# Whole-row runs for the weight loads of a decode block: wq, w_mod, w1 and w2 as consecutive rows per partition, activations transposed with a matching step

## Chip, cores, metric

One core of one Trainium2 chip. The metric is device microseconds of one execution. Of the 29 executions of the kernel before that are on record, 28 lie within 0.3% (703.12 to 704.98 us; the other took 706.48); a verdict of "faster" or "slower" needs 2%. A ratio below is the mean time of one kernel's fast runs over that of the other kernel's fast runs of the same rounds, so it is not quite the ratio of the medians that stand beside it.

In this document, MB are 10^6 bytes and KB 1024 bytes. Shares of a microsecond are read from single traces unless medians are named; traces of kernels with the same beginning agree there within about 0.3 us (w_mod's product starts at 21.27 to 21.59 us in five traces).

## The reference, cut to what matters

A transformer block in decode: 8 sequences, one new token each, D = 512, 32 query heads on 8 key/value heads, 8192 cached keys of 128 numbers, an MLP of 1792 hidden units with squared ReLU, all bf16.

```python
mod = silu(c) @ w_mod                      # [8,512] @ [512,3072] -> sa, ca, ga, sb, cb, gb
h = layernorm(x) * (1 + ca) + sa
q = h @ wq                                 # [8,512] @ [512,4096]
p = softmax(q . k_cache * Dh**-0.5)        # k_cache, v_cache: [8, 8, 8192, 128] each, 134 MB each
x = x + ga * ((p . v_cache) @ wo)          # wo: [4096,512]
h = layernorm(x) * (1 + cb) + sb
x = x + gb * (relu(h @ w1 + b1)**2 @ w2 + b2)   # w1: [512,1792], w2: [1792,512]
```

The caches are 268 MB of the 284 MB read. The four weights of the change are 11 MB.

## The kernel before

K and V come in 128 loads of 2 MB through a ring of eight slots, each partition getting one run of 16 KB. wq and w_mod borrow ring slots 6, 7 and 4, 5 at the start; w1 and w2 are the last two loads. PE (TensorE, the matrix engine; PEld is its loading of weights) transposes K, multiplies it with the queries, transposes the softmaxed scores P and multiplies them with V; VectorE and ScalarE (DVE and ACT in the profile) copy PE's results out.

The parts that the change touches:

```python
RING = [E0(nc.sbuf_tensor(f"ring{i}", [128, NT, DH], BF16)) for i in range(NSLOT)]
# ...
wq_r = A_wq.rearrange("(kt p) n -> p kt n", p=128)         # row kt*128+p on partition p
s_wq.inc(sp.dma_start(RINGF[6]..., wq_r[:, 0:2, :]), 16)    # 2 runs of 8 KB per partition
s_xc.inc(sp.dma_start(x_sb[:], A_x...), 16)
s_xc.inc(sp.dma_start(c_sb[:], c), 16)
s_wq.inc(sp.dma_start(RINGF[7]..., wq_r[:, 2:4, :]), 16)
wmod_r = w_mod.rearrange("(kt p) n -> p kt n", p=128)      # runs of 6 KB, two DMAs
# ...
for kt in range(KT_D):      # transposes of silu(c); the same for the two normalized rows, ha and hb
    ins = pe.matmul(csT_tp[:, kt, :], cs[:, kt * 128:(kt + 1) * 128], IDENT[0:B, 0:B], is_transpose=True)
# ...
for m in range(NLOADS):     # the load queue: wait for the slot, then issue
    # ... K, V: "(p t) d -> p t d", one run of 16 KB per partition
    # m == 4 also issues wo: A_wo.rearrange("(h dh) n -> dh h n"), 32 runs of 1 KB per partition
    # m == 128: B_w1.rearrange("(kt p) f -> p kt f", p=128)     4 runs of 3.5 KB
    # m == 129: B_w2.rearrange("(kt p) n -> p kt n", p=128)    14 runs of 1 KB
# ...
for hh, (f0, fl) in enumerate(FH):          # the hidden row, in two halves of 896
    s_dve.wait(pe, M_HSQH[hh])
    for kt in range(f0 // 128, (f0 + fl) // 128):
        ins = pe.matmul(hidT_tp[:, kt, :], hsq[:, kt * 128:(kt + 1) * 128], IDENT[0:B, 0:B], is_transpose=True)
    if hh == 0:
        pe_fill(pe, 10)                     # "fillers": matmuls whose result nobody reads
```

Of the kernel before, what the change touches and what calls it, by code (L numbers as in the profile page):

```python
# [9 lines left out]
BF16 = mybir.dt.bfloat16  # L10
# [17 lines left out]
def bass_adaLN_cond__gqa_block_cached__dense_activation_squared_relu__decode_kernel(  # L28
    nc, A_x, A_k_cache, A_v_cache, A_wq, A_wo, B_x, B_w1, B_b1, B_w2, B_b2, c, w_mod, out):
    B, _, D = A_x.shape  # L30
    _, HKV, SK, DH = A_k_cache.shape
    HQ = A_wq.shape[1] // DH
    REP = HQ // HKV
    F = B_w1.shape[1]
    NMOD = w_mod.shape[1]
    KT_D = D // 128
    KT_F = F // 128
    NCH = SK // 512
    NT = SK // 128
    NSLOT = 8  # L40
# [5 lines left out]
    with ExitStack() as es0:  # L46
        E0 = es0.enter_context
# [6 lines left out]
        IDENT = E0(nc.sbuf_tensor("IDENT", [128, 128], BF16))  # L54
# [21 lines left out]
        mv = E0(nc.sbuf_tensor("mv", [B, 2], FP32))  # L76
        std_ = E0(nc.sbuf_tensor("std_", [B, 1], FP32))
        rstd = E0(nc.sbuf_tensor("rstd", [B, 1], FP32))
        RING = [E0(nc.sbuf_tensor(f"ring{i}", [128, NT, DH], BF16)) for i in range(NSLOT)]
        RINGF = [r[:, :, :].rearrange("p t d -> p (t d)") for r in RING]  # L80

        WQ_SLOTS = (6, 7)
        WMOD_SLOTS = (4, 5)

        def wq_view(kt, h):
            r = RINGF[WQ_SLOTS[kt // 2]]
            base = (kt % 2) * (HQ * DH) + h * DH
            return r[:, base:base + DH]

        def wmod_view(kt, j):  # L90
            r = RINGF[WMOD_SLOTS[kt // 2]]
            base = (kt % 2) * NMOD + j * 512
            return r[:, base:base + 512]

        PS = E0(nc.psum_tensor("PS", [128, 8, 512], FP32))
        mod_ps = PS[0:B, 0:6, :]
# [1 line left out]
        csT_tp = tpro[:, 0:KT_D * B].rearrange("p (k b) -> p k b", k=KT_D)  # L98
        haT_tp = tpro[:, 32:32 + KT_D * B].rearrange("p (k b) -> p k b", k=KT_D)
# [12 lines left out]
        hbT_tp = PS[:, 7, :].bitcast(BF16)[:, 128:128 + KT_D * B].rearrange("p (k b) -> p k b", k=KT_D)  # L112
        hid_ps = PS[0:B, 0:4, :]
        hid_flat = hid_ps.rearrange("b k n -> b (k n)")
        hidT_tp = PS[:, 7, :].bitcast(BF16)[:, 0:KT_F * B].rearrange("p (k b) -> p k b", k=KT_F)
# [4 lines left out]
        s_wmod = S_("s_wmod")  # L120
        s_wq = S_("s_wq")
# [26 lines left out]
        def slot_of(m):  # L148
            return m % NSLOT, m // NSLOT

        def load_kind(m):
            if m >= 128:
                return ("w", m, 0)
            b, r = divmod(m, 16)
            return ("k", b, r) if r < 8 else ("v", b, r - 8)
        def v_uses_before(m):
            s = m % NSLOT
            return sum(1 for mm in range(s, m, NSLOT) if load_kind(mm)[0] == "v")

        def stg_k(b, g, j):  # L160
            return 72 * b + 8 * g + j
# [15 lines left out]
        def wait_evac(eng, seq):  # L177
            e, v = evac_ms[seq]
            (s_edve if e == "dve" else s_eact).wait(eng, v)
# [14 lines left out]
        cs = E1(nc.sbuf_tensor("cs", [B, D], BF16))  # L194
# [3 lines left out]
        ha = E1(nc.sbuf_tensor("ha", [B, D], BF16))  # L198
        haT = E1(nc.sbuf_tensor("haT", [128, KT_D, B], BF16))

        @block.sync
        def _(sp):
            wq_r = A_wq.rearrange("(kt p) n -> p kt n", p=128)
            s_wq.inc(sp.dma_start(RINGF[WQ_SLOTS[0]].rearrange("p (k n) -> p k n", k=2), wq_r[:, 0:2, :]), 16)
            s_xc.inc(sp.dma_start(x_sb[:], A_x.rearrange("b s d -> (b s) d")), 16)
            s_xc.inc(sp.dma_start(c_sb[:], c), 16)
            s_wq.inc(sp.dma_start(RINGF[WQ_SLOTS[1]].rearrange("p (k n) -> p k n", k=2), wq_r[:, 2:4, :]), 16)
            wmod_r = w_mod.rearrange("(kt p) n -> p kt n", p=128)
            s_wmod.inc(sp.dma_start(RINGF[WMOD_SLOTS[0]][:, 0:2 * NMOD].rearrange("p (k n) -> p k n", k=2), wmod_r[:, 0:2, :]), 16)
            s_wmod.inc(sp.dma_start(RINGF[WMOD_SLOTS[1]][:, 0:2 * NMOD].rearrange("p (k n) -> p k n", k=2), wmod_r[:, 2:4, :]), 16)  # L210
        V_XC = s_xc.n

        @block.gpsimd
# [57 lines left out]
        @block.tensor  # L271
        def _(pe):
            s_dve.wait(pe, M_CS)
            s_pool.wait(pe, M_CONSTS)
            for kt in range(KT_D):
                ins = pe.matmul(csT_tp[:, kt, :], cs[:, kt * 128:(kt + 1) * 128], IDENT[0:B, 0:B], is_transpose=True)  # L276
            s_pe.inc(ins)
        M_TPC = s_pe.n

# [33 lines left out]
        @block.tensor  # L313
        def _(pe):
            s_dve.wait(pe, M_HA)
            for kt in range(KT_D):
                ins = pe.matmul(haT_tp[:, kt, :], ha[:, kt * 128:(kt + 1) * 128], IDENT[0:B, 0:B], is_transpose=True)
            s_pe.inc(ins)
        M_TPH = s_pe.n

# [43 lines left out]
        @block.sync  # L364
        def _(sp):
            for m in range(NLOADS):
                s, u = slot_of(m)
                kind = load_kind(m)
                if u == 0:
                    if s in WQ_SLOTS:  # L370
                        s_pe.wait(sp, M_QT)
                    elif s in WMOD_SLOTS:
                        s_pe.wait(sp, M_MODMM)
                    if m == 4:
                        s_wo.inc(sp.dma_start(wo_sb[:], A_wo.rearrange("(h dh) n -> dh h n", dh=DH)), 16)
                        s_bb.inc(sp.dma_start(b1_row[:], B_b1.rearrange("(o f) -> o f", o=1)), 16)
                        s_bb.inc(sp.dma_start(b2_row[:], B_b2.rearrange("(o f) -> o f", o=1)), 16)
                else:
                    pk = load_kind(m - NSLOT)
                    if pk[0] == "k":  # L380
                        wait_evac(sp, stg_k(pk[1], pk[2], 7))
                    else:
                        assert pk[0] == "v"
                        s_free[s].wait(sp, v_uses_before(m))
                if kind[0] == "k":
                    src_ap = A_k_cache[kind[1], kind[2]].rearrange("(p t) d -> p t d", p=128)
                    dst_ap = RING[s][:, :, :]
                elif kind[0] == "v":
                    src_ap = A_v_cache[kind[1], kind[2]].rearrange("(p t) d -> p t d", p=128)
                    dst_ap = RING[s][:, :, :]  # L390
                elif m == LD_W1:
                    src_ap = B_w1.rearrange("(kt p) f -> p kt f", p=128)
                    dst_ap = W1v
                else:
                    src_ap = B_w2.rearrange("(kt p) n -> p kt n", p=128)
                    dst_ap = W2v
                ins = sp.dma_start(dst_ap, src_ap)
                if kind[0] in ("k", "v"):
                    s_ld[s].inc(ins, 16)
                elif m == LD_W1:  # L400
                    s_w1.inc(ins, 16)
                else:
                    s_w2.inc(ins, 16)
# [23 lines left out]
        for b in range(B):  # L427
            def T_tile(pe, b_, g_, j0=0, j1=8):
# [4 lines left out]
                for j in range(j0, j1):  # L433
# [3 lines left out]
                    for i in range(8):  # L437
                        t = 8 * j + i
                        ins = pe.matmul(STG[seq % NSTG][:, i, :], RING[s][:, t, :], IDENT[:, :], is_transpose=True)  # L439
                    v = s_stgw.inc(ins)  # L440
# [127 lines left out]
            def PV_group(pe, g):  # L568
# [6 lines left out]
                for t in range(NT):  # L575
                    if g == 0 and t % 8 == 0:
# [3 lines left out]
                                    Pm[:, t, 32 * qt + REP * g:32 * qt + REP * (g + 1)],  # L580
                                    RING[s][:, t, :], start=(t == 0), stop=(t == NT - 1),
                                    tile_position=(0, 32 * gq))
# [101 lines left out]
        hb = E3(nc.sbuf_tensor("hb", [B, D], BF16))  # L684
        hbT = E3(nc.sbuf_tensor("hbT", [128, KT_D, B], BF16))
        h1 = E3(nc.sbuf_tensor("h1", [B, F], BF16))
        hsq = E3(nc.sbuf_tensor("hsq", [B, F], BF16))
# [6 lines left out]
        def pe_fill(pe, n):  # L694
            for _ in range(n):
                pe.matmul(EFILL_ps, IDENT[:, :], IDENT[:, :])
# [33 lines left out]
        @block.tensor  # L730
        def _(pe):
            pe_fill(pe, 48)
            s_dve.wait(pe, M_HB)
            for kt in range(KT_D):
                ins = pe.matmul(hbT_tp[:, kt, :], hb[:, kt * 128:(kt + 1) * 128], IDENT[0:B, 0:B], is_transpose=True)
            s_pe.inc(ins)
            pe_fill(pe, 6)
        M_HBT = s_pe.n
# [34 lines left out]
        @block.tensor  # L773
        def _(pe):
            for hh, (f0, fl) in enumerate(FH):
                s_dve.wait(pe, M_HSQH[hh])
                for kt in range(f0 // 128, (f0 + fl) // 128):
                    ins = pe.matmul(hidT_tp[:, kt, :], hsq[:, kt * 128:(kt + 1) * 128], IDENT[0:B, 0:B], is_transpose=True)
                if hh == 0:
                    pe_fill(pe, 10)  # L780
            s_pe.inc(ins)
            pe_fill(pe, 6)
        M_HIDT = s_pe.n
# [59 lines left out]
```

## Time and profile before

| | before |
|---|---|
| time, median of 4 runs | 703.39 us (703.12 to 704.98) |
| bytes moved, packets | 285 MB, 26,109 |
| PE busy | 88% |
| last K load lands | 635.4 us |
| from there to the end | 66.3 us |

From the page of the kernel before: the span, PE's busy time, then two rows of 40 equal slices (busy share of the DMA engines in tenths, and GB/s), the packets by size, and the queue that fetches instructions.

```profile
span 701.7 us, 21480 instructions
PE 617.2 (88%) x10113; PEld 528.0 (75%) x10113; DVE 324.6 (46%) x594; ACT 177.7 (25%) x217; POOL 6.2 (1%) x25
...
DMA  9999999999999999999999999999999999999950
GB/s 354 430 372 429 423 427 425 424 425 428 428 423 425 427 427 424 427 425 426 425 425 426 425 427 423 428 427 424 427 425 425 423 430 424 426 426 427 412 208 1
DMA packets 26109, 285.05 MB, mean 406 GB/s; under 512 B 2187, under 2 KB 8100, under 8 KB 9125
...
q8 instruction: 80, 1.31, 0.8%
```

The DMA engines have no dry slice from the first to the last two. Note slice 2 (372 GB/s): that is where wo's 1 KB runs go through.

The view by stretches of the kernel before, stretches in us. The last two columns are the share of the DMA engines' time that was busy (over 1 where the times of packets overlap) and GB/s.

```profile
core 0: us, PE busy (x) PEld busy (x) DVE busy (x) ACT busy (x) POOL busy (x), PEclk, DMA share, GB/s
4.00:21.00 17.00, 0.26 (x4) 0.18 (x4) 2.09 (x6) 2.11 (x3) 3.13 (x13) 1.00 1.02 425
41.00:51.00 10.00, 10.00 (x147) 8.46 (x145) 7.57 (x12) 3.46 (x4) 0.00 (x0) 0.86 1.09 346
52.00:652.00 600.00, 546.85 (x9106) 473.57 (x9104) 298.03 (x530) 167.67 (x206) 0.00 (x0) 0.97 1.01 425
668.00:683.00 15.00, 15.00 (x257) 13.65 (x254) 1.85 (x9) 0.00 (x0) 0.00 (x0) 1.00 0.54 205
```

In the last row, w1 and w2 go through while only half of the DMA engines' time is used.

The chain of waits of the kernel before, in order of time (start, duration, what). These are two of its pieces: the wait for the last K load, and PE's first work on it.

```profile
598.51 36.87 DMA ring<-in_A_k_cache_dram
635.43 1.96 PE PS L439 x32
```

A piece of DMA in the chain runs from issue to landing, so it contains the time that the load stood in the queue. It ends at 598.51 + 36.87 = 635.38 us. Here the queue is never empty (no dry slice above), so the issue time does not matter (in experiment 7 PE starts on K 1.7 us later, and the last K lands at 634.75 us instead of 634.72); what matters is how much has to go through before.

The beginning, in the timeline of the kernel before (start, duration, engine, line, operation; in brackets the idle time before and what ended it):

```profile
9.02 0.63 ACT L244 ACTIVATE sig<-c_sb 8x512 f32<-8x512 bf16 x1 [6.93 <-DMA c_sb<-in_c_dram]
10.42 0.26 PE L276 MATMUL PS<-IDENT,cs 8*128 8x8 bf16 x4 [10.42 <-DVE cs L250]
21.33 8.02 PE L292 MATMUL PS<-ring,csT 128*8 128x512 bf16 x24 [10.65 <-DMA ring<-in_w_mod_dram]
```

PE waits for w_mod until 21.3 us; the activations were ready by 12.

The end, in the timeline of the kernel before: the second half of the squared hidden row, PE's transposes of the hidden row with ten fillers between, and VectorE's copy of the result.

```profile
693.55 0.61 DVE L771 TENSOR_TENSOR hsq<-h 8x896 bf16<-8x896 bf16 x1 [0.69 <-ACT h L766]
...
693.95 0.33 PE L778 MATMUL PS<-IDENT,hsq 8*128 8x8 bf16 x7
...
694.21 0.73 PE L696 MATMUL PS<-IDENT 128*128 128x128 bf16 x10
...
694.87 0.33 PE L778 MATMUL PS<-IDENT,hsq 8*128 8x8 bf16 x7
...
695.23 0.22 DVE L788 COPY hidT<-PS 128x112 bf16<-128x112 bf16 x1 [1.07 <-PE PS L778]
```

### The profile page before, as it was taken

The numbers are of one execution on the slowest core, as the hardware profiler recorded it, in microseconds if no ns is written. First come the engines' busy times: TensorE is split into PE (matmuls) and PEld (weight loads), VectorE is DVE, ScalarE is ACT, GpSimd is POOL, SyncE is SP. The second block draws the span as 40 slices with busy tenths as digits, with TensorE's granted clock in tenths as the row PEclk, the third lists the DMA queues.
The fourth block names the chain that finished last, engine by engine and source line by source line (L and its number), as shares of the span: only waits on it lengthen the run. The fifth ranks groups of instructions, "written<-read, shape, count | busy, mean of one in ns | idle before, by whom it ended". The sixth has DMA issues, their size and how long they took to land.

```text
span 701.7 us, 21480 instructions
## 1 busy us (share of the span) xinstructions
PE 617.2 (88%) x10113; PEld 528.0 (75%) x10113; DVE 324.6 (46%) x594; ACT 177.7 (25%) x217; POOL 6.2 (1%) x25
## 2 busy tenths in 40 slices
PE   0499799997989799997999899897989989997998
PEld 0187699776977699776987699776977689775984
DVE  1357612774057621766046720676027820676213
ACT  1024510443024410433013320344014420244101
POOL 3000000000000000000000000000000000000000
PEclk9979999999999899999999989999999999999999
DMA  9999999999999999999999999999999999999950
GB/s 354 430 372 429 423 427 425 424 425 428 428 423 425 427 427 424 427 425 426 425 425 426 425 427 423 428 427 424 427 425 425 423 430 424 426 426 427 412 208 1
DMA packets 26109, 285.05 MB, mean 406 GB/s; under 512 B 2187, under 2 KB 8100, under 8 KB 9125
## 3 DMA queue, kind: packets, MB, share of 16 engines
q1 hardware_dynamic: 26020, 283.68, 96.2%
q8 instruction: 80, 1.31, 0.8%
q14 instruction: 9, 0.07, 0.0%
HBM read 283.66 MB, written 0.01 MB: 404 GB/s over the span
## 4 chain that ended last, share of the span: by engine, by line
PE 49%; DMA 38%; DVE 10%; ACT 2%; issue 1%; SPq 0%
DMA ring<-in_A_k_cache_dram 30%; PE PS L439 23%; PE PS L579 14%; PE PS L477 6%; DMA ring<-in_A_v_cache_dram 5%; DVE KTb L413 5%; DMA ring<-in_w_mod_dram 3%; DVE m L501 2%; ACT P_sb L528 2%; PE PS L551 2%; PE PS L292 1%; PE PS L634 1%; PE PS L333 1%; DVE mod_sb L300 0%; PE PS L796 0%
## 5 line engine op out<-in xcount | busy, mean ns | idle before, releaser
L413 DVE COPY KTb<-PS 128x1024 bf16<-128x1024 bf16 x432 | 270.9, 684 | 80.7 <-PE PS L439 79.8
L439 PEld LDWEIGHTS PS<-IDENT,ring 128*128 128x128 bf16 x4096 | 230.7, 98 | 63.1 <-DMA ring<-in_A_k_cache_dram 35.3
L439 PE MATMUL PS<-IDENT,ring 128*128 128x128 bf16 x4096 | 251.2, 220 | 12.9 <-DMA ring<-in_A_k_cache_dram 11.8
L420 ACT ACTIVATE KTb<-PS 128x1024 bf16<-128x1024 bf16 x144 | 147.5, 1024 | 445.2 <-PE PS L439 423.5
L579 PE MATMUL PS<-ring,KTb 128*4 128x128 bf16 x4096 | 221.6, 219 | 8.8 <-DVE rinv L563 5.3
L579 PEld LDWEIGHTS PS<-ring,KTb 128*4 128x4 bf16 x4096 | 218.3, 85 | 10.7 <-DVE rinv L563 6.2
L596 DVE CAST O_sb<-PS 128x256 bf16<-128x256 f32 x7 | 3.0, 425 | 196.3 <-PE PS L579 196.3
L477 PE MATMUL PS<-KTb,QTm 128*32 128x512 bf16 x1024 | 78.8, 384 | 5.3 <-ACT KTb L420 5.3
L551 PE MATMUL PS<-IDENT,P_sb 128*128 128x128 bf16 x512 | 45.1, 271 | 10.2 <-ACT P_sb L528 10.0
L551 PEld LDWEIGHTS PS<-IDENT,P_sb 128*128 128x128 bf16 x512 | 42.8, 126 | 11.8 <-ACT P_sb L528 10.7
L477 PEld LDWEIGHTS PS<-KTb,QTm 128*32 128x32 bf16 x1024 | 15.7, 94 | 21.5 <-DVE KTb L413 9.0
L528 ACT ACTIVATE P_sb<-PS,negm 128x512 bf16<-128x512 f32 x32 | 21.5, 685 | 22.9 <-DVE negm L519 22.9
L501 DVE TENSOR_REDUCE m<-PS 128x1 f32<-128x512 f32 x32 | 19.8, 680 | 0.0
L292 PE MATMUL PS<-ring,csT 128*8 128x512 bf16 x24 | 8.0, 511 | 10.6 <-DMA ring<-in_w_mod_dram 10.6
L609 DVE CAST O_sb<-PS 4x128 bf16<-4x128 f32 x8 | 2.3, 287 | 26.6 <-PE PS L579 26.6
L292 PEld LDWEIGHTS PS<-ring,csT 128*8 128x8 bf16 x24 | 2.5, 107 | 15.7 <-issue 14.6
L511 PEld LDWEIGHTS PS<-Dm,R 128*128 128x128 bf16 x8 | 0.8, 96 | 17.3 <-DVE Dm L505 17.3
L511 PE MATMUL PS<-Dm,R 128*128 128x4 bf16 x8 | 1.4, 179 | 13.3 <-DVE Dm L505 13.3
L535 DVE TENSOR_REDUCE rs<-rs 128x1 f32<-128x4 f32 x8 | 1.3, 157 | 22.8 <-ACT P_sb L528 22.8
L300 DVE CAST mod_sb<-PS 8x3072 bf16<-8x3072 f32 x1 | 3.3, 3345 | 17.5 <-PE PS L292 17.5
L276 PE MATMUL PS<-IDENT,cs 8*128 8x8 bf16 x4 | 0.3, 167 | 10.4 <-DVE cs L250 10.4
L715 ACT ACTIVATE std_<-std_ 8x1 f32<-8x1 f32 x1 | 0.2, 202 | 34.5 <-DVE std_ L709 34.5
(87 smaller groups left out, 98.9 us busy)
## 6 DMA issues: line engine op xcount, KB each, us to landing
ring<-in_A_k_cache_dram SPq DMA_DIRECT2D x64, 2048.0 KB, 30.7
ring<-in_A_v_cache_dram SPq DMA_DIRECT2D x64, 2048.0 KB, 35.0
ring<-in_A_wq_dram SPq DMA_DIRECT2D x2, 2048.0 KB, 9.7
wo_sb<-in_A_wo_dram SPq DMA_DIRECT2D x1, 4096.0 KB, 24.7
ring<-in_B_w_dram SPq DMA_DIRECT2D x2, 1792.0 KB, 24.9
ring<-in_w_mod_dram SPq DMA_DIRECT2D x2, 1536.0 KB, 16.5
x_sb<-in_A_x_dram SPq DMA_DIRECT2D x1, 8.0 KB
c_sb<-in_c_dram SPq DMA_DIRECT2D x1, 8.0 KB
```

The lines of the kernel that those rows point to most:

```text
L292: ins = pe.matmul(mod_ps[:, j, :], csT[:, kt, :], wmod_view(kt, j), start=(kt == 0), stop=(kt == KT_D - 1))
L300: s_dve.inc(dve.tensor_copy(mod_sb[:], mod_ps.rearrange("b k n -> b (k n)")))
L333: ins = pe.matmul(QT_ps[:, h, :], wq_view(kt, h), haT[:, kt, :], start=(kt == 0), stop=(kt == KT_D - 1))
L413: v = s_edve.inc(dve.tensor_copy(dst, STG[seq % NSTG]))
L420: v = s_eact.inc(act.activation(dst, STG[seq % NSTG], ACT.Copy))
L439: ins = pe.matmul(STG[seq % NSTG][:, i, :], RING[s][:, t, :], IDENT[:, :], is_transpose=True)
L477: ins = pe.matmul(S_ps[32 * q:32 * (q + 1), k, :], QTm[:, b, g, :], KTb[:, 512 * cch:512 * (cch + 1)], start=(g == 0), stop=(g == HKV - 1) ...
L501: s_dve.inc(dve.tensor_reduce(m4[:, k:k + 1], S_ps[:, k, :], AX.X, ALU.max))
L528: ins = act.activation(P_sb[:, k, :], S_ps[:, k, :], ACT.Exp, bias=negm[:, 0:1], scale=inv_sqrt, accum_out=rs4[:, k:k + 1])
L551: ins = pe.matmul(STG[seq % NSTG][:, i, :], P_sb[:, k, j0:j0 + 128], IDENT[:, :], is_transpose=True)
L579: ins = pe.matmul(Ob[32 * gq:32 * gq + REP, co:co + 128], Pm[:, t, 32 * qt + REP * g:32 * qt + REP * (g + 1)], RING[s][:, t, :], start=(t ...
L634: ins = pe.matmul(attn_ps, oTn[:, h, :], wo_view(h), start=(h == 0), stop=(h == HQ - 1))
```

## The change

Intent: fewer and longer runs. With rows (p k) instead of (k p), partition p holds rows p*K to p*K+K-1, which are one run in HBM: 32 KB for wq, 24 KB for w_mod, 14 KB for w1 and for w2. A product over rows does not care which rows form a group, as long as the activations are grouped alike, so each transpose now takes columns with a step of 4 (rows of 512) or 14 (rows of 1792). The ring becomes one tensor, so that a run may cross a slot's border, and wq and w_mod need one DMA each. A group of the hidden row now has columns of both halves, so its 14 transposes all wait for the second half.

```diff
-        RING = [E0(nc.sbuf_tensor(f"ring{i}", [128, NT, DH], BF16)) for i in range(NSLOT)]
+        RALL = E0(nc.sbuf_tensor("rall", [128, NSLOT, NT, DH], BF16))
+        RING = [RALL[:, i, :, :] for i in range(NSLOT)]
+        RFLAT = RALL[:, :, :, :].rearrange("p s t d -> p (s t d)")
   ... (the views of wq and w_mod follow)
-            wq_r = A_wq.rearrange("(kt p) n -> p kt n", p=128)
-            s_wq.inc(sp.dma_start(RINGF[WQ_SLOTS[0]]..., wq_r[:, 0:2, :]), 16)
+            s_wq.inc(sp.dma_start(RFLAT[:, wq0:wq0 + KT_D * HQ * DH], A_wq.rearrange("(p k) n -> p (k n)", k=KT_D)), 16)
             s_xc.inc(sp.dma_start(x_sb[:], A_x.rearrange("b s d -> (b s) d")), 16)
             s_xc.inc(sp.dma_start(c_sb[:], c), 16)
-            s_wq.inc(sp.dma_start(RINGF[WQ_SLOTS[1]]..., wq_r[:, 2:4, :]), 16)
-   ... (two DMAs of w_mod)
+            s_wmod.inc(sp.dma_start(RFLAT[:, wm0:wm0 + KT_D * NMOD], w_mod.rearrange("(p k) n -> p (k n)", k=KT_D)), 16)
   ... (likewise for ha and hb)
-                ins = pe.matmul(csT_tp[:, kt, :], cs[:, kt * 128:(kt + 1) * 128], IDENT[0:B, 0:B], is_transpose=True)
+                ins = pe.matmul(csT_tp[:, kt, :], cs[:, :].rearrange("b (p k) -> b k p", k=KT_D)[:, kt, :], IDENT[0:B, 0:B], is_transpose=True)
   ...
-                    src_ap = B_w1.rearrange("(kt p) f -> p kt f", p=128)
+                    src_ap = B_w1.rearrange("(p kt) f -> p kt f", p=128)
-                    src_ap = B_w2.rearrange("(kt p) n -> p kt n", p=128)
+                    src_ap = B_w2.rearrange("(p kt) n -> p kt n", p=128)
   ...
                 s_dve.wait(pe, M_HSQH[hh])
-                for kt in range(f0 // 128, (f0 + fl) // 128):
-                    ins = pe.matmul(hidT_tp[:, kt, :], hsq[:, kt * 128:(kt + 1) * 128], IDENT[0:B, 0:B], is_transpose=True)
                 if hh == 0:
                     pe_fill(pe, 10)
+                for kt in range(KT_F) if hh == 1 else ():
+                    ins = pe.matmul(hidT_tp[:, kt, :], hsq[:, :].rearrange("b (p k) -> b k p", k=KT_F)[:, kt, :], IDENT[0:B, 0:B], is_transpose=True)
```

More of the change, by code (lines that the diff above doesn't have):

```diff
@@ L78, in bass_adaLN_cond__gqa_block_cached__dense_activation_squared_relu__decode_kernel @@
         rstd = E0(nc.sbuf_tensor("rstd", [B, 1], FP32))
-        RING = [E0(nc.sbuf_tensor(f"ring{i}", [128, NT, DH], BF16)) for i in range(NSLOT)]
-        RINGF = [r[:, :, :].rearrange("p t d -> p (t d)") for r in RING]
+        RALL = E0(nc.sbuf_tensor("rall", [128, NSLOT, NT, DH], BF16))
+        RING = [RALL[:, i, :, :] for i in range(NSLOT)]
+        RINGF = [r.rearrange("p t d -> p (t d)") for r in RING]
+        RFLAT = RALL[:, :, :, :].rearrange("p s t d -> p (s t d)")
         WQ_SLOTS = (6, 7)
@@ L85, in wq_view @@
         def wq_view(kt, h):
-            r = RINGF[WQ_SLOTS[kt // 2]]
-            base = (kt % 2) * (HQ * DH) + h * DH
-            return r[:, base:base + DH]
+            base = WQ_SLOTS[0] * NT * DH + kt * (HQ * DH) + h * DH
+            return RFLAT[:, base:base + DH]
         def wmod_view(kt, j):
-            r = RINGF[WMOD_SLOTS[kt // 2]]
-            base = (kt % 2) * NMOD + j * 512
-            return r[:, base:base + 512]
+            base = WMOD_SLOTS[0] * NT * DH + kt * NMOD + j * 512
+            return RFLAT[:, base:base + 512]
         PS = E0(nc.psum_tensor("PS", [128, 8, 512], FP32))
@@ L202, in _ @@
         def _(sp):
-            wq_r = A_wq.rearrange("(kt p) n -> p kt n", p=128)
-            s_wq.inc(sp.dma_start(RINGF[WQ_SLOTS[0]].rearrange("p (k n) -> p k n", k=2), wq_r[:, 0:2, :]), 16)
+            wq0, wm0 = WQ_SLOTS[0] * NT * DH, WMOD_SLOTS[0] * NT * DH
+            s_wq.inc(sp.dma_start(RFLAT[:, wq0:wq0 + KT_D * HQ * DH], A_wq.rearrange("(p k) n -> p (k n)", k=KT_D)), 16)
             s_xc.inc(sp.dma_start(x_sb[:], A_x.rearrange("b s d -> (b s) d")), 16)
             s_xc.inc(sp.dma_start(c_sb[:], c), 16)
-            s_wq.inc(sp.dma_start(RINGF[WQ_SLOTS[1]].rearrange("p (k n) -> p k n", k=2), wq_r[:, 2:4, :]), 16)
-            wmod_r = w_mod.rearrange("(kt p) n -> p kt n", p=128)
-            s_wmod.inc(sp.dma_start(RINGF[WMOD_SLOTS[0]][:, 0:2 * NMOD].rearrange("p (k n) -> p k n", k=2), wmod_r[:, 0:2, :]), 16)
-            s_wmod.inc(sp.dma_start(RINGF[WMOD_SLOTS[1]][:, 0:2 * NMOD].rearrange("p (k n) -> p k n", k=2), wmod_r[:, 2:4, :]), 16)
+            s_wmod.inc(sp.dma_start(RFLAT[:, wm0:wm0 + KT_D * NMOD], w_mod.rearrange("(p k) n -> p (k n)", k=KT_D)), 16)
         V_XC = s_xc.n
@@ L316, in _ @@
             for kt in range(KT_D):
-                ins = pe.matmul(haT_tp[:, kt, :], ha[:, kt * 128:(kt + 1) * 128], IDENT[0:B, 0:B], is_transpose=True)
+                ins = pe.matmul(haT_tp[:, kt, :], ha[:, :].rearrange("b (p k) -> b k p", k=KT_D)[:, kt, :], IDENT[0:B, 0:B], is_transpose=True)
             s_pe.inc(ins)
@@ L734, in _ @@
             for kt in range(KT_D):
-                ins = pe.matmul(hbT_tp[:, kt, :], hb[:, kt * 128:(kt + 1) * 128], IDENT[0:B, 0:B], is_transpose=True)
+                ins = pe.matmul(hbT_tp[:, kt, :], hb[:, :].rearrange("b (p k) -> b k p", k=KT_D)[:, kt, :], IDENT[0:B, 0:B], is_transpose=True)
             s_pe.inc(ins)
```

## The prediction

> **What bounds the kernel now.** The DMA queue. By the stretches view it moves 425 GB/s with its engines fully busy from 52 to 652 us; the page's GB/s row shows no dry slice until the last two. PE is nearly balanced with it (88% busy), so the chain of waits alternates between PE work and K loads, but PE freeing a slot earlier only lengthens the queue. The last K load lands at 635.4 us; from there PE's own work runs some 66 us to the end.
>
> **What changes.**
> 1. wq and w_mod: 1024 runs of 8 and 6 KB become 256 runs of 32 and 24 KB; four DMAs become two. [...] This trace agrees for the 1 KB runs of wo: about 346 GB/s (41 to 51 us). Estimate from that: 4096 runs over 16 engines, 12.1 us instead of 9.9, some 8.5 ns per run and engine; for 48 runs fewer per engine, 0.4 us. But wq and w_mod already move at 425 GB/s (4 to 21 us), like the 16 KB runs of K and V, so the gain is likelier 0 to 0.4 us; it counts fully, being time of the bottleneck.
> 2. w1 and w2: 3.5 and 1 KB runs become 14 KB. By the same estimate, about 1 us of queue time, but worth nothing: their last bytes land near 683 us, and the MLP's products start at 689.4 (w1) and 695.6 us (w2), released by VectorE copies, not by a DMA. Slack 6 us or more.
> 3. x and c now queue behind 4 MB of wq instead of 2: their landing (9.0 us, when the sigmoid starts) moves to about 14. Sigmoid, norm and transposes took until 12.0, so are ready about 17; PE waits for w_mod until 21.3 us. Hidden.
> 4. Transposes of the hidden row: the first 7 of 14 can no longer run before the second half of the square. Before: 7 transposes, 10 fillers, 7 transposes (693.95 to 695.2 us); now 10 fillers, then 14 transposes. PE had no gap there, and the second half (ready 694.2) is in time for the end of the fillers (about 694.6): same PE work, same end.
> 5. Strided weight loads: 26 loads of 8x128 now step 8 bytes (28 for the hidden row's 14). [...] Before, the 14 issue every 35 ns. If a strided load costs 50 to 100 ns, the hidden row loses 0.2 to 0.9 us on the tail chain; the 8-byte ones next to nothing.
>
> **Sum.** −0.2 (DMA head), +0.3 (tail), other moves hidden: no measurable change. Predicted **703.3 us**, range **701.3 to 705.3**. Faster by over 2%: 0.02; within 2%: 0.96; slower by over 2%: 0.02.
>
> **What would show it.** Step 1: GB/s of the first slices unchanged, w_mod's product starting between 20.6 and 21.4 us. Step 2: the DMA row falls off up to 1 us earlier; the MLP's products still wait for VectorE. Step 3: the sigmoid at 13 to 15 us. Step 4: 10 fillers, then 14 transposes, no idle gap over 0.2 us before them. Step 5: the 14 spaced above 35 ns. Last K landing within 1 us of 635.4; packets from 26,109 to some 23,300.
>
> **What would make it wrong.** Runs of 32 KB moving slower or less evenly over the 16 engines; x and c landing after w_mod; the engines' uneven finish (DMA share 0.54 in 668 to 683 us) being caused by the short runs, so that the pace of the slowest engine, which sets the K landings, improves by more than I count.

The sum comes to −0.2 + 0.3 = +0.1 us. The first term is the estimate from wo's rate in the trace of before (346 GB/s against 425), and "this trace agrees" in step 1 means no more than that. The second rests on the assumption of 50 to 100 ns for a strided load, for which no run had given a number yet, and on a spacing of 35 ns, where the trace of before shows 25. Measured later: 60 ns and +0.49 us for the 28-byte step (experiment 4), and 90 to 112 ns for a weight load with the 8-byte step.

## The result, and the profile after

703.25 us, median of 4 runs (703.07 to 703.81), against 703.39 of before: ratio 0.9994, 95% interval 0.998 to 1.0008. No difference in time is measured. The traces show two small movements that nearly cancel: the last K load lands 0.7 us sooner, and the stretch from there to the end is 0.4 us longer.

The page of the changed kernel:

```profile
span 701.4 us, 21478 instructions
...
GB/s 375 429 371 425 425 426 424 428 426 424 425 426 424 428 425 423 427 427 426 426 425 421 427 429 422 425 427 426 426 426 422 426 429 425 424 427 426 422 188 1
DMA packets 23260, 285.05 MB, mean 406 GB/s; under 512 B 2154, under 2 KB 6275, under 8 KB 6276
```

2849 packets fewer, the same GB/s. (The GB/s view books a packet's bytes where the packet starts, so the first slice with its 32 KB packets, 375 instead of 354, looks better than it is.)

Stretches of the changed kernel:

```profile
4.00:21.00 17.00, 0.73 (x6) 0.38 (x7) 2.09 (x6) 2.11 (x3) 3.10 (x13) 1.00 0.98 422
...
52.00:652.00 600.00, 545.75 (x9111) 472.95 (x9109) 297.62 (x530) 168.17 (x206) 0.00 (x0) 0.97 1.01 426
668.00:683.00 15.00, 15.00 (x248) 13.26 (x245) 1.93 (x9) 0.00 (x0) 0.00 (x0) 1.00 0.45 187
```

Chain of waits of the changed kernel; the load lands at 597.89 + 36.83 = 634.72 us:

```profile
597.89 36.83 DMA rall<-in_A_k_cache_dram
```

The beginning in its timeline. The sigmoid of c starts 4.4 us later, since c stands behind twice as much of wq; w_mod's product starts 0.77 us sooner all the same.

```profile
13.43 0.63 ACT L241 ACTIVATE sig<-c_sb 8x512 f32<-8x512 bf16 x1 [11.35 <-DMA c_sb<-in_c_dram]
14.82 0.29 PE L273 MATMUL PS<-IDENT,cs 8*128 8x8 bf16 x4 [14.82 <-DVE cs L247]
20.56 8.27 PE L289 MATMUL PS<-rall,csT 128*8 128x512 bf16 x24 [5.45 <-DMA rall<-in_w_mod_dram]
```

The end in its timeline. From the end of the second square to VectorE's copy, 1.07 us have become 1.38 (the bracket of the last line):

```profile
691.89 2.07 PE L693 MATMUL PS<-IDENT 128*128 128x128 bf16 x34
...
692.93 0.61 DVE L768 TENSOR_TENSOR hsq<-h 8x896 bf16<-8x896 bf16 x1 [0.69 <-ACT h L763]
693.89 1.00 PE L777 MATMUL PS<-IDENT,hsq 8*128 8x8 bf16 x14
...
694.92 0.22 DVE L785 COPY hidT<-PS 128x112 bf16<-128x112 bf16 x1 [1.38 <-PE PS L777]
```

Ahead of the 14 transposes PE runs 24 + 10 fillers without a gap, as foreseen. The transposes themselves are slower. The view of one line's instructions shows their weight loads (durations min/median/max in ns), of the kernel before and then of the changed one:

```profile
L778 PEld LDWEIGHTS PS<-IDENT,hsq x14: 90/91/94, 693.9 to 695.0; 8*128 8x128 bf16 x14
```

```profile
L777 PEld LDWEIGHTS PS<-IDENT,hsq x14: 133/154/155, 693.9 to 694.6; 8*128 8x128 bf16 x14
```

### The profile page after: what moved, and what is told of

It is laid out like the page before. It is cut to its first block, busy times and chain, and to the rows that moved or that the text cites. A ratio compares the mean times of both kernels' runs of the same rounds, so it can differ in the third digit from the quotient of the medians.

```text
span 701.4 us, 21478 instructions
## 1 busy us (share of the span) xinstructions
PE 616.6 (88%) x10113; PEld 527.9 (75%) x10113; DVE 324.5 (46%) x594; ACT 177.7 (25%) x217; POOL 6.1 (1%) x25
## 2 busy tenths in 40 slices
DMA packets 23260, 285.05 MB, mean 406 GB/s; under 512 B 2154, under 2 KB 6275, under 8 KB 6276
## 4 chain that ended last, share of the span: by engine, by line
PE 48%; DMA 38%; DVE 11%; ACT 3%; issue 0%; SPq 0%
DMA rall<-in_A_k_cache_dram 30%; PE PS L436 23%; PE PS L576 13%; PE PS L474 6%; DVE KTb L410 5%; DMA rall<-in_A_v_cache_dram 5%; DMA rall<-in_w_mod_dram 3%; ACT P_sb L525 3%; DVE m L498 2%; PE PS L289 1%; PE PS L548 1%; PE PS L631 1%; PE PS L330 1%; DVE mod_sb L297 0%; PE PS L793 0%
## 5 line engine op out<-in xcount | busy, mean ns | idle before, releaser
L436 PEld LDWEIGHTS PS<-IDENT,rall 128*128 128x128 bf16 x4096 | 230.8, 98 | 62.5 <-DMA rall<-in_A_k_cache_dram 34.7
L436 PE MATMUL PS<-IDENT,rall 128*128 128x128 bf16 x4096 | 251.3, 220 | 12.5 <-DMA rall<-in_A_k_cache_dram 11.6
L417 ACT ACTIVATE KTb<-PS 128x1024 bf16<-128x1024 bf16 x144 | 147.4, 1024 | 440.2 <-PE PS L436 419.0
L576 PE MATMUL PS<-rall,KTb 128*4 128x128 bf16 x4096 | 221.7, 219 | 9.6 <-DVE rinv L560 5.2
L576 PEld LDWEIGHTS PS<-rall,KTb 128*4 128x4 bf16 x4096 | 218.4, 85 | 11.5 <-DVE rinv L560 6.1
L474 PEld LDWEIGHTS PS<-KTb,QTm 128*32 128x32 bf16 x1024 | 15.7, 94 | 21.4 <-DVE KTb L410 9.0
L508 PE MATMUL PS<-Dm,R 128*128 128x4 bf16 x8 | 1.4, 178 | 13.4 <-DVE Dm L502 13.4
L289 PE MATMUL PS<-rall,csT 128*8 128x512 bf16 x24 | 8.3, 524 | 5.4 <-DMA rall<-in_w_mod_dram 5.4
L289 PEld LDWEIGHTS PS<-rall,csT 128*8 128x8 bf16 x24 | 2.6, 110 | 10.7 <-issue 9.7
## 6 DMA issues: line engine op xcount, KB each, us to landing
rall<-in_w_mod_dram SPq DMA_DIRECT2D x1, 3072.0 KB, 18.4
```

The lines of the kernel that those rows point to most:

```text
L289: ins = pe.matmul(mod_ps[:, j, :], csT[:, kt, :], wmod_view(kt, j), start=(kt == 0), stop=(kt == KT_D - 1))
L417: v = s_eact.inc(act.activation(dst, STG[seq % NSTG], ACT.Copy))
L436: ins = pe.matmul(STG[seq % NSTG][:, i, :], RING[s][:, t, :], IDENT[:, :], is_transpose=True)
L474: ins = pe.matmul(S_ps[32 * q:32 * (q + 1), k, :], QTm[:, b, g, :], KTb[:, 512 * cch:512 * (cch + 1)], start=(g == 0), stop=(g == HKV - 1) ...
L576: ins = pe.matmul(Ob[32 * gq:32 * gq + REP, co:co + 128], Pm[:, t, 32 * qt + REP * g:32 * qt + REP * (g + 1)], RING[s][:, t, :], start=(t ...
```

## The experiments

Ten kernels ran, in three groups, each with its own runs of the kernel before. Theory: the DMA queue bounds the kernel; every packet has a small fixed cost (measured below: 9.0 ns at 8 KB, 8.6 at 1 KB), so fewer packets ahead of the last K load save exactly their own cost; the tail gives part of it back through the strided weight loads; everything else is hidden. The rivals stand with each run.

### 1. The head alone

The changed kernel with w1, w2, hb's and the hidden row's transposes put back.

```diff
-                    src_ap = B_w1.rearrange("(p kt) f -> p kt f", p=128)
+                    src_ap = B_w1.rearrange("(kt p) f -> p kt f", p=128)
   (likewise w2, hb, and the two halves of the hidden row)
```

> The change for wq and w_mod alone; w1, w2 and the transposes of the MLP as in the kernel before. Theory (long runs at the head save time of the bottleneck, the tail loses a little to strided weight loads): w_mod's product starts near 20.6 us instead of 21.3, the last K load lands near 634.7 us instead of 635.4, the hidden row's transposes issue every 35 ns again, and the time is 702.7 us, 0.7 below before and 0.3 to 0.5 below the changed kernel. Rival (the head gained nothing, 0.7 us is the scatter of single traces): last K at 635.4, time equal to before within 0.2 us.

702.91 us against 703.79 of before (5 runs; ratio 0.9986, 0.9973 to 0.9998). Its timeline and its chain:

```profile
20.62 7.84 PE L289 MATMUL PS<-rall,csT 128*8 128x512 bf16 x24 [5.52 <-DMA rall<-in_w_mod_dram]
```

```profile
598.04 36.86 DMA rall<-in_A_k_cache_dram
```

The last K lands at 634.9 us, the rest takes 66.3 us as before. The gain of the head shows in the landing of the last K and, just, in the interval of the time (with one run of before at 706.48 us in it). It is the larger of the change's two gains (the other is in experiment 4). Of the correct kernels this one has the lowest ratio, some 0.1% below before, though its interval overlaps that of the changed kernel.

### 2. The tail alone

The kernel before with the new rows of w1 and w2 and the strided transposes of the MLP.

```diff
-                    src_ap = B_w2.rearrange("(kt p) n -> p kt n", p=128)
+                    src_ap = B_w2.rearrange("(p kt) n -> p kt n", p=128)
   (likewise w1, hb, and the block of 14 transposes)
```

> The change for w1 and w2 alone, with the strided transposes of the MLP and the block of 14; the head as before. Theory: the last K load lands at 635.4 us as before, the last weight DMA ends about 1 us earlier, the MLP's products still wait for VectorE, and the stretch from the last K landing to the end grows by 0.3 to 0.5 us; time 703.8. Rival (long runs of w1 and w2 are worth their queue time): time 702.4.

703.92 us against 703.79 (5 runs; ratio 0.9998, 0.9986 to 1.0011). Chain and end of the timeline:

```profile
598.59 36.86 DMA ring<-in_A_k_cache_dram
```

```profile
696.18 0.22 DVE L788 COPY hidT<-PS 128x112 bf16<-128x112 bf16 x1 [1.39 <-PE PS L780]
```

The last K lands as before (635.45 us), the last increment of w2's semaphore comes at 683.1 us instead of 683.8, and that 0.7 us buys nothing. VectorE's copy again comes 1.39 us after the second square. From the last K to the end this trace took 67.2 us, 0.5 us more than the strided loads explain; in it PE's clock fell to half for longer just after the last K (granted 0.50 in all of 643 to 649 us, where before was back at 0.75 by 647 to 649), and the 64 transposes of P took 6.1 us instead of 5.4. Two other traces, with the old tail, show the same longer half-clock stretch (experiment 6: 0.50 in 643 to 647 us and 0.59 to 649; experiment 8: 0.50 in 645 to 651). It is scatter of the clock, not an effect of the change, and as large as what is studied here.

### 3. One DMA each, but short runs

As experiment 1, with the old rows: one DMA of 8 KB runs for wq, one of 6 KB runs for w_mod.

```diff
-... A_wq.rearrange("(p k) n -> p (k n)", k=KT_D)
+... A_wq.rearrange("(k p) n -> p k n", p=128)
   (likewise w_mod; unit-step transposes of c and of the first normalized row)
```

> wq and w_mod with one DMA each, in the changed kernel's order, but with the old rows: runs of 8 and 6 KB, contiguous transposes; MLP as before. Theory (the saving comes from fewer packets, each with a fixed cost of about 12 ns, as the packets' times by size suggest): w_mod's product starts near 21.2 us, last K lands at 635.2 to 635.4, time 703.3. Rival (it comes from two DMAs fewer, or from x and c standing behind wq): 20.6 us, 634.7 and 702.7, like the head alone.

703.47 us against 703.79 (ratio 0.9993, 0.998 to 1.0006).

```profile
21.07 8.02 PE L289 MATMUL PS<-rall,csT 128*8 128x512 bf16 x24 [5.69 <-DMA rall<-in_w_mod_dram]
```

```profile
598.31 36.86 DMA rall<-in_A_k_cache_dram
```

In between. The last K lands at 635.17 us; with the old head it was 635.39 and 635.45 (before, experiment 2), with the new head 634.72, 634.90, 634.77 and 634.75 (after, experiments 1, 4 and 7), mean 634.79. So the longer runs are worth about 0.4 us, and two DMAs fewer, or the other order, about 0.25. The split rests on this one trace, and the four traces with the new head differ by 0.18 us among themselves, so both parts are rough. What the quarter microsecond consists of was not settled. The 12 ns of the expectation are an estimate from median packet times in the trace of before (49 ns at 1 KB, 613 at 16 KB, a straight line through both). Neither theory as expected was quite right: the theory gave all to the runs, the rival nothing.

### 4. Unit-step columns in the block of 14

The changed kernel with other columns transposed; wrong result.

```diff
-   hsq[:, :].rearrange("b (p k) -> b k p", k=KT_F)[:, kt, :]
+   hsq[:, kt * 128:(kt + 1) * 128]
```

> The changed kernel with the hidden row's 14 transposes reading unit-step columns, in the same place after the 10 fillers; wrong result on purpose. Theory (the step of 28 bytes slows the weight load): they issue every 35 ns instead of 66, a weight load takes 90 ns instead of 154, and VectorE's copy of the transposed hidden row starts about 0.45 us sooner after the second square. Rival (the block of 14 itself, or where it stands, is what is slower): spacing stays near 66 ns.

One look, state unknown: 702.73 us. End of its timeline:

```profile
694.04 0.50 PE L777 MATMUL PS<-IDENT,hsq 8*128 8x8 bf16 x14
...
694.58 0.22 DVE L785 COPY hidT<-PS 128x112 bf16<-128x112 bf16 x1 [0.89 <-PE PS L777]
```

The block takes 0.50 us instead of 1.00, and the copy comes 0.89 us after the square instead of 1.38. In the records of the traces the transposes start 25 ns apart, as in the kernel before, where the changed kernel has 60; the 35 and 66 ns of the expectation (and the 35 of the prediction) were misread, while their difference is nearly right. So the step of 28 bytes costs 0.49 us. Against the kernel before (1.07) the new order, fillers first, is even 0.18 us better. Net: 0.31 us lost.

### 5. Twice the packets for K and V

The kernel before with K and V in runs of 8 KB: the same bytes, 16,384 more packets, 1024 for each of the 16 engines on average.

```diff
-   A_k_cache[kind[1], kind[2]].rearrange("(p t) d -> p t d", p=128)
+   A_k_cache[kind[1], kind[2]].rearrange("(a p u) d -> p a u d", p=128, u=32)   (then (u d) joined)
   (likewise V)
```

> The kernel before with the K and V loads in runs of 8 KB instead of 16 (two runs per partition; keys renumbered alike in K and V, so the result stays right). 1024 more packets for each of the 16 engines. Theory (each packet has a fixed cost, so run length counts wherever the DMA queue is the bottleneck): by the packets' median times in the trace of before (309 ns for 8 KB, 613 for 16 KB) 5 ns per packet, so 5.1 us: last K near 640.5, time 708.5. The estimate of the prediction from wo's runs (8.5 ns) gives 8.7 us and 712. Rival (runs of 8 KB are as good as 16, which the 425 GB/s of the head seemed to say): 703.4 within 0.5 us.

712.62 us against 703.60 (ratio 1.0127, 1.011 to 1.0143). Stretch and chain:

```profile
60.00:630.00 570.00, 518.23 (x8586) 449.84 (x8579) 269.44 (x479) 150.86 (x184) 0.00 (x0) 0.97 1.01 419
```

```profile
610.29 34.36 DMA ring<-in_A_k_cache_dram
```

The last K lands 9.26 us later, at 644.65: 9.0 ns per packet. The estimate of the prediction (8.5 ns from wo) holds; the smaller number from the packets' median durations (5 ns; in this experiment's own trace they would give 13) and the rival (none) do not. Which places of memory a load reads changed together with the number of packets; that experiment 6, with quite other runs, comes to nearly the same cost speaks for the number. Over 570 us, 8 KB runs move at 419 GB/s and 16 KB runs at 425. The 17 us of the head, from which the prediction read "the same 425", cannot show such a difference: with the very same head this stretch reads 419 in this trace and 428 in that of experiment 6.

### 6. wo in one run per partition

The kernel before with wo's 4096 packets of 1 KB made 128 of 32 KB; wrong result, since the projection then meets other rows.

```diff
-   A_wo.rearrange("(h dh) n -> dh h n", dh=DH)
+   A_wo.rearrange("(dh h) n -> dh h n", dh=DH)
```

> The kernel before with wo's 4 MB loaded as one 32 KB run per partition instead of 32 runs of 1 KB; wrong result on purpose, since the projection then meets other rows. Theory (short runs cost most where they are really short and before the last K load): by median packet times 256 x 49 ns less 8 x 1213 ns per engine, 2.8 us: last K near 632.6, time 700.5. Rival (the time of wo hides behind PE's work): 703.4.

702.34 us against 703.60 (ratio 0.9983, 0.9965 to 1.0001; 701.1 to 704.2). Stretch and chain:

```profile
41.00:51.00 10.00, 10.00 (x146) 8.84 (x144) 7.09 (x12) 3.07 (x3) 0.00 (x0) 0.83 1.00 423
```

```profile
596.56 36.70 DMA ring<-in_A_k_cache_dram
```

wo now moves at 423 GB/s instead of 346, and the last K lands 2.13 us sooner (633.26): 248 packets fewer per engine, 8.6 ns each. Again the prediction's estimate (2.2 us) is nearer than the median durations (2.8). This trace too has the long half-clock stretch after the last K (67.2 us to the end), which hides part of the gain in its time. The largest saving by longer runs that was found here lies in wo, which the change does not touch. Its layout ties partition to the number within a head, and no correct version of this was tried.

### 7. x and c after w_mod

The changed kernel with x and c issued last of the head.

```diff
+            s_wmod.inc(sp.dma_start(... w_mod ...), 16)
             s_xc.inc(sp.dma_start(x_sb[:], ...), 16)
             s_xc.inc(sp.dma_start(c_sb[:], c), 16)
-            s_wmod.inc(sp.dma_start(... w_mod ...), 16)
```

> The changed kernel with x and c issued after w_mod instead of before it. They land near 21 us instead of 13, so sigmoid, c's transposes and w_mod's product slip to about 24.5 us, and PE's first K transpose from 39.8 to about 43.5. Theory (the DMA queue is the bottleneck, PE's start is not): the last K load lands at 634.7 us as in the changed kernel and the time is 703.3, within 0.5 us. Rival (PE's chain of work sets the time): 3 to 4 us more, 707.

703.36 us against 703.86 (ratio 0.9995, 0.9978 to 1.0011). From its timeline, and its chain:

```profile
23.59 6.91 PE L289 MATMUL PS<-rall,csT 128*8 128x512 bf16 x24 [1.22 <-DVE csT L280]
...
41.43 4.87 PE L436 MATMUL PS<-IDENT,rall 128*128 128x128 bf16 x44 [0.97 <-DVE QTm L342]
```

```profile
597.89 36.87 DMA rall<-in_A_k_cache_dram
```

w_mod's product now waits for VectorE, 3.0 us later; PE's first K transpose starts at 41.4 us instead of 39.8 (a smaller delay than expected, since the product and what follows it ran faster). The last K lands at 634.75 us, as in the changed kernel. PE's start does not matter: the DMA queue decides.

### 8. More instructions to fetch

Half of the DMA engines' time is idle at the end (share 0.54 in 668 to 683 us), and the 16 increments of a load's semaphore drift apart. The trace shows 16 updates for a 128-partition load, and 9 for each of the 8-partition loads of x and c: one early (1.80 and 2.19 us) and eight when the load lands (8.28 to 9.00 us). That an increment tells of one of the 16 DMA engines is the reading, here and below; the trace names no engine. Read from the semaphores of the traces, the time from the first to the last of the 16, every eighth load:

```
before            0.7  2.0  3.6  3.6  5.1  6.7  6.7  8.3  8.3  9.8 11.4 11.4 13.0 13.0 14.5 16.1
changed           0.5  2.0  3.2  3.4  4.9  6.3  6.5  7.9  8.0  9.6 11.2 11.1 12.7 12.7 14.2 15.8
more code         1.9 10.0 16.3 16.3 16.3 16.3 16.3 16.2 16.3 16.2 16.2 16.2 16.2 16.2 16.2 16.2
less code         0.6  1.8  3.1  3.3  3.6  4.9  5.2  6.5  6.8  8.0  8.3  9.6  9.9 11.1 11.4 12.7
```

The drift is the same in the changed kernel, so the short runs of the weights did not cause it. It grows in ten steps of some 1.55 us, and there are 80 instruction fetches of 16 KB: one step for every eight (from this and from the two groups that follow comes the theory of the expectation, eight engines and 1.55 us for each fetch). Sorted, the 16 increments of the last K load are two groups: eight within 4.3 us of the first, eight from 14.2 to 16.1 us after it. Experiment 8 adds 3072 one-byte memsets on GpSimd to the kernel before.

```diff
+            for i in range(3072):
+                pool.memset(SCR[0:1, i:i + 1], 0)
```

> The kernel before with 3072 tiny memsets (one partition, one byte each[...]) on GpSimd behind its constants: some 190 KB more of instructions to fetch, 12 more fetch packets of 16 KB beside the 80. Theory (the instruction fetches go to 8 of the 16 DMA engines in turn, each costs its engine about 1.55 us, and these 8 set the landing of K): the spread between the first and the last of a load's 16 semaphore increments grows from 16.1 us to about 18.4 at the end, the last K lands near 637.7, time 705.7. Rival (the uneven engines have another cause, such as data or short runs): spread and time as before.

704.33 us against 703.60 (ratio 1.0013, 0.9998 to 1.0027); last K 636.67 us, 1.3 later. The drift rises early, while GpSimd works, and then stays at 16.3. The additional fetches, 23 packets of 8 KB or 184 KB, came on another queue (32 packets on it instead of 9), not among the 80 of q8, whose count stayed. (The expectation's 12 packets are an estimate from the trace of before: 80 of 16 KB for 20,226 instructions of PE, 65 bytes each.) From its DMA view:

```profile
q14 instruction: 32, 0.26, 0.1%
```

Sorted, the increments show what the drift alone hides. From the 17th load on, one single increment is 16.3 us late, while the other fifteen go on much as before (all within 2.2 us there; at the last K seven within 4.8 us and eight from 13.0 to 14.4 us). These packets passed between 13 and 129 us, and the one increment fell behind in that time only: an estimate from 16.3 us and 23 more packets is 0.7 us each. So with more code an increment does come late, here a single one, which reads as one engine by itself; the expected sizes (18.4 us, 637.7 us) were wrong, since they put the fetches on eight engines.

### 9. wo in pieces, meant to shift load off the engines taken to be late

Experiment 1 with wo's partitions 48 to 127 loaded by ten DMAs of 8 partitions.

```diff
-   s_wo.inc(sp.dma_start(wo_sb[:], wo_r), 16)
+   s_wo.inc(sp.dma_start(wo_sb[0:48, :, :], wo_r[0:48]), 16)
+   for p0 in range(48, 128, 8):
+       s_wo.inc(sp.dma_start(wo_sb[p0:p0 + 8, :, :], wo_r[p0:p0 + 8]), 16)
```

> The head-alone kernel with wo's load split: partitions 0 to 47 in one DMA over 16 engines, partitions 48 to 127 in ten DMAs of 8 partitions[...]. Correct result. Theory (8 engines run late by 16 us because of instruction fetches): if the 8 engines of the pieces are the ones without fetches, some 8 us of load moves from the late to the early ones: spread at the end near 0, last K near 627, time 695. If they are the same ones, the late ones get 8 us more: last K 643, spread 32, time 711. Rival (no such lasting difference between engines): spread and time as in the head-alone kernel, 702.9, or a little worse.

753.17 us against 703.60 (ratio 1.069). A failure for a reason that no theory named. Its GB/s row:

```profile
GB/s 375 430 134 59 87 255 426 427 425 424 427 428 425 424 425 427 423 426 428 426 426 425 424 426 426 426 427 426 426 424 429 422 427 426 427 424 426 415 220 3
```

While the pieces go through, the queue moves 59 GB/s; the 1 KB packets took a median of 145 ns instead of 49. Why loads of eight neighbouring partitions move so slowly was not shown. Later the drift starts from 5.4 us and still grows by the usual steps to 18.8. That does not mean that the pieces ran on the eight engines taken to be late. (That a piece runs on eight engines and the first load on 16 is again a reading: the page counts 80 packets under 512 B more than that of the changed kernel, 2234 against 2154, eight for each of the ten pieces if the first load has as many as the whole one.) Sorted, the increments of the last K load come at 0 to 0.2 us (two), 4.5 to 8.2 us (six), 12.1 to 14.2 us (six) and 18.7 to 18.8 us (two). Read as engines, the same eight would all have ended near 19; this looks like two sets of eight that have two engines in common, which neither case of the expectation allowed for. The increments carry no engine's name, so this is inferred from their order.

### 10. Fewer instructions to fetch

The kernel before with every second tile of P times V left out: 4096 PE instructions fewer, all loads the same; wrong result.

```diff
-                for t in range(NT):
+                for t in range(0, NT, 2):
```

> The kernel before with only every second of the 64 tiles of P times V computed; wrong result on purpose. 4096 PE instructions fewer, all loads the same. Theory (fetch packets of 16 KB load 8 of the 16 DMA engines, and these set the landing of K): fetch packets fall from 80 to 64, the spread of a load's 16 increments at the end from 16.1 us to about 13, the last K lands some 3.1 us earlier, near 632.3, beside what the shorter P times V takes off the tail. Rival (the uneven landing has another cause): spread 16.1 and last K 635.4 as before; the tail alone gets shorter.

695.40 us against 703.86 (ratio 0.9879, 0.9865 to 0.9894), most of it from the shorter tail. The fetch queue of its DMA view:

```profile
q8 instruction: 64, 1.05, 0.6%
```

PE, in its timeline, gets the last K load at 632.48 us, where it was 635.43 before:

```profile
632.48 1.79 PEld L439 LDWEIGHTS PS<-IDENT,ring 128*128 128x128 bf16 x32 [0.45 <-DMA ring<-in_A_k_cache_dram]
```

The drift of the last K load is 12.7 us instead of 16.1, and it lands at 632.43 us, 2.95 sooner, as expected (13 and 3.1). Its bytes of K, V and weights are unchanged and the queue stayed full. PE also had less work, but experiment 7 showed that PE's timing does not move the last K, and here the first of its 16 increments came no sooner (619.7 us, before 619.3); only the late group moved. So instruction fetches do set part of the pace: 16 fewer are worth 3 us here, more than four times the whole head of the change.

## Why the prediction was right, point by point

- **The bound.** Right. A PE start 1.7 us later left the last K where it was (experiment 7); packets added to or taken from the queue moved it by their own cost (5, 6).
- **Step 1, the head.** That fewer packets save time there and the 8.5 ns per packet were right: 9.0 (experiment 5) and 8.6 ns (6) when measured with a lever. The term of the sum was too small: −0.2 us was put down, the traces show −0.64 (mean of the new heads against the old), of which 0.4 from the runs and 0.25 from fewer DMAs or their order. The wording that was off is "But wq and w_mod already move at 425 GB/s ... so the gain is likelier 0 to 0.4 us": 17 us are too short to read 1.5% of a rate, and the saving from merged DMAs was not counted. For the same reason w_mod's product started at 20.56 us, just ahead of the foretold 20.6 to 21.4.
- **Step 2, w1 and w2.** Right. Their last bytes come 0.7 us sooner by experiment 2 alone, and the MLP's products wait for VectorE in all traces.
- **Step 3, x and c.** Right: the sigmoid at 13.4 us, hidden. Even 3 us behind w_mod would have been hidden.
- **Step 4, the block of 14.** Right as to "no gap", slightly wrong as to "same end": fillers first saves 0.18 us (experiment 4).
- **Step 5, strided weight loads.** Right, and inside its range: the spacing went from 25 ns (not 35, as the prediction read) to 60, 0.49 us for the 14. The 8-byte step costs little, as said: VectorE's copy after hb's four transposes waits 0.39 us instead of 0.34. A weight load of 8x128 bf16 took a median of 90 (hb) or 91 ns (hidden row) with unit step, 112 with a step of 8 bytes (hb) and 154 with 28 (hidden row).
- **Sum.** −0.64 at the head and +0.36 in the tail give −0.28 us; the two profiled spans differ by 0.30 us. Predicted: −0.2 + 0.3. The first term was off by 0.44 us, the second by 0.06. The stated 703.3 us does not follow from the prediction's own sum, which gives +0.1 us and so 703.5; that it lies 0.05 us from the measured median is luck. The forecast "within 2%" would also have been met with every rival tested on this change, so it is the traces, and not the time, that bear out the steps.
- **The stated doubt** about the uneven engines: real as a bound, but not caused by the short runs (the increments of a load near the end spread over 16.1 us before and 15.8 in the changed kernel). Its cause is at least in part instruction fetch (experiments 8 and 10: with 64 fetches on q8 instead of 80 the spread is 12.7 us, and the last K lands 2.95 us sooner).

## What to carry to other kernels

Before making runs longer, count packets per DMA engine ahead of the load that the critical path waits for last, and multiply by the cost per packet measured where runs are really short; median packet durations mislead about it (for wo they gave 2.8 us, where the queue lost 2.1). Here the same change after that load was worth nothing (experiment 2), and from 8 KB up it takes many packets to be worth something before it (0.4 us for 48 per engine here, 9.3 us for 1024). Where a DMA-bound kernel has thousands of small PE instructions, look at its instruction fetches as traffic too (here 16 fetches of 16 KB fewer brought the last K load 2.95 us sooner). A layout change for loads is paid in another place: here a step of 28 bytes in 14 small weight loads cost 0.49 us, about what 48 packets per engine had saved.
